# The merge of the key-value blocks into wo: from 48 split matmuls to 64 small float32 ones

## The chip, the cores and the metric

The kernel runs on one core of one Trainium2 chip. The metric is the device time of one execution in microseconds; a kernel's figure is the median of its runs.

## The reference

A linear-attention block and a gated feed-forward block share one input x of 2048 rows and 1024 columns, and the output joins them:

```python
xn = layernorm(x)
q, k, v = heads(xn @ wqkv)               # 32 heads of 32 columns
pq, pk = phi(q), phi(k)                  # phi(t) = t + 1 if t > 0 else exp(t), + 1e-6
kv  = einsum("hsd,hse->hde", pk, v)      # 32 x 32 for each head
den = einsum("hqd,hd->hq", pq, pk.sum(s)) + 1e-6
s = concat(pq @ kv / den) @ wo           # wo is 1024 x 1024
g = silu((silu(x @ w1) * (x @ w3)) @ w2) # 3584 hidden columns
out = x + s * g
```

All is float32. Since the division by den is by row and head, `(pq @ kv / den) @ wo` is `(pq / den) @ M`, where the 32 rows of M that belong to head h are `kv[h] @ wo[32h:32h+32]`. The kernel computes M, "the merge", once, and multiplies by it later.

## The kernel before

**Products.** The large products are made of 2x2 block products in seven multiplications (A11, S1 to S4, A12, A22 on one side; B11, B21, B22, T1 to T4 on the other). Each float32 operand is split into a high and a low part of the type fp32r: `split` casts on ACT (ScalarE) and subtracts on DVE (VectorE). `mm3` then multiplies high by high, high by low, low by high: three matmuls of 128x128 by 128x512 on PE (TensorE), the lines L109, L110 and L111.

**Order of the work.** The main line of the program is the projections and the two halves of the feed-forward block. Beside it runs a list of side jobs: `catch_up`, called at marks between products, takes one step of the first job of the list each time (a step ends at a `yield`). `go_on` runs a list of jobs one after another and has the loads of two jobs asked ahead. A job's tiles come from `job_tile`, one ring of four buffers; PSUM banks from `bank`, eight of them; split operands from `operand`, six. From the resulting program a scheduler sets the order of each engine's queue. All side jobs' loads and stores in question are issued by SP (SyncE).

**The stage of the change.** `attention_work` first divides 8 pieces of pq by den; then, for k = 0 to 3 and e = 0, 1, runs the pair `key_values(j)`, merge of j, with j = k + 4e (four heads, 128 rows of M each); then divides the other 24 pieces; then come sums of weights.

- `key_values(j)` loads g, the columns of xn^T pk that belong to four heads (an earlier product, 512 KB, L1309), and the same heads' columns of wqkv for v, wv (512 KB, L1312). L1323 makes the four heads' blocks, wv^T g, with 32 float32 matmuls that contract 128 of the 1024 rows each and have 32 columns, in four column tiles: `tile_position=(0, g * DH)`. The result is 128x32 in a bank `kv`: four 32x32 blocks stacked. L1327 multiplies on DVE with the 0/1 mask `hmask`, which spreads them to a 128x128 tile `kvf` with four blocks on the diagonal and zeros elsewhere.
- `merge_wo(k)` loads 128 rows of wo (L1340, 512 KB) for each e, splits `kvf` to `kvm`, and the two halves of wo's rows to `wos`, runs `mm3` into `wp` for each half, and copies the bank back over the rows of wo (L1356, ACT). After e = 1 it stores the four quarter blocks and their sums (`sums_of`, on POOL, lines L1145 to L1149) as 7 operands to `wp_d` (L1369, 256 KB each). The product by M loads `wp_d` (as `wpr`) some 300 us later.

The denominators (`den`, L1258) appear in the prediction for comparison: float32 matmuls in four column tiles of 128x32, with 256 columns each.

Of the kernel before, what the change touches and what calls it, by code (L numbers as in the profile page):

```python
# [9 lines left out]
F32 = mybir.dt.float32  # L10
FR = mybir.dt.float32r
# [5 lines left out]
P = 128  # L17
C = 512
# [4 lines left out]
def tile_linear_attention_times_swiglu(  # L23
# [10 lines left out]
    nc = tc.nc  # L34
    x, out = x[0], out[0]
    S, D = x.shape
    F = w1.shape[1]
    ND = D // P
# [52 lines left out]
    YS = ["Y00", "Y01", "Y10", "R5", "R2", "R4", "R6"]  # L91
    x_d = [dram.tile([P, TH // 2, len(XS), C], F32, name=f"x_d{h}") for h in range(NH)]
    y_d = [dram.tile([P, TH // 2, len(YS), ND // 2, P], F32, name=f"y_d{h}") for h in range(NH)]
    g_d = [dram.tile([P, ND // 2, C], F32, name=f"g_d{n}") for n in range(4)]
    a_d = {n: dram.tile([P, 2, ND // 2, C], F32, name=f"a_d{n}") for n in AOPS}

    def split(pair, src, negated=False):

        hi, lo = pair if isinstance(pair, tuple) else (pair[:, 0], pair[:, 1])
        if negated:  # L100
            nc.scalar.mul(hi, src, -1.0)  # L101
            return nc.vector.scalar_tensor_tensor(lo, src, -1.0, hi.bitcast(F32), op0=ALU.mult, op1=ALU.subtract)  # L102
        nc.scalar.copy(out=hi, in_=src)  # L103
        return nc.vector.tensor_sub(out=lo, in0=src, in1=hi.bitcast(F32))  # L104

    def mm3(acc, w, a, start, stop):

        (wh, wl), (ah, al) = w, a
        nc.tensor.matmul(acc, lhsT=wh, rhs=ah, start=start, stop=False, skip_group_check=True)  # L109
        nc.tensor.matmul(acc, lhsT=wh, rhs=al, start=False, stop=False, skip_group_check=True)  # L110
        return nc.tensor.matmul(acc, lhsT=wl, rhs=ah, start=False, stop=stop, skip_group_check=True)  # L111
# [10 lines left out]
    st = era1.enter_context(tc.tile_pool(name="st", bufs=2))  # L122
# [19 lines left out]
    def job_tile(shape, name):  # L142
        return praw.tile(shape, F32, tag="job", bufs=4, name=name)
# [66 lines left out]
    class Opening:  # L210
# [653 lines left out]
    def half(h):  # L864
# [47 lines left out]
        else:  # L912
# [318 lines left out]
    def go_on(work, ahead=2):  # L1231

        data = [j.load() for j in work[:ahead]]
        for i, j in enumerate(work):
            yield from j.steps(data[i])
            if i + ahead < len(work):
                data.append(work[i + ahead].load())
# [61 lines left out]

        return Job(load, steps)  # L1300

    kvf = {}

    def key_values(j):

        def load():
            g = job_tile([P, 2, ND // 2, P], f"g{j}")
            for e in range(2):
                nc.sync.dma_start(out=g[:, e], in_=g_d[2 * e + j % 2][:, :, j // 2 * P:(j // 2 + 1) * P])  # L1309
            w = job_tile([P, 2, ND // 2, P], f"wv{j}")  # L1310
            rows = wqkv[:, 2 * D + j * P:2 * D + (j + 1) * P]
            nc.sync.dma_start(out=w.rearrange("p e k n -> p (e k) n"), in_=rows.rearrange("(k p) n -> p k n", p=P))  # L1312
            return g, w

        def steps(both):
            yield True
            acc = bank(f"kv{j}")[:, :DH]
            g_, w_ = both
            for e in range(2):
                for k in range(ND // 2):  # L1320
                    for g in range(P // DH):
                        c = slice(g * DH, (g + 1) * DH)
                        nc.tensor.matmul(acc[c], lhsT=w_[:, e, k, c], rhs=g_[:, e, k, c], skip_group_check=True,  # L1323
                                         start=e + k == 0, stop=bool(e) and k == ND // 2 - 1, tile_position=(0, g * DH))
# [6 lines left out]
        return [Job(load, steps)]  # L1331

    def merge_wo(k):

        both = []

        def load(e):
            j = k + e * (ND // 2)
            t = job_tile([P, 2, C], f"wo{j}")
            nc.sync.dma_start(out=t, in_=wo[j * P:(j + 1) * P, :].rearrange("p (n c) -> p n c", c=C))  # L1340
            return t

        def steps(e, t):
            both.append(t)
            j = k + e * (ND // 2)
            kvm = st.tile([P, 2, P], FR, tag="kvm", bufs=1, name=f"kvm{j}")
            split(kvm, kvf[j])
            o = []
            for n in range(2):
                o.append(operand([P, 2, C], FR, f"wos{j}_{n}"))  # L1350
                split(o[n], t[:, n])
                yield True
            for n in range(2):
                acc = bank(f"wp{j}_{n}")
                mm3(acc, (kvm[:, 0], kvm[:, 1]), (o[n][:, 0], o[n][:, 1]), True, True)
                nc.scalar.copy(out=t[:, n], in_=acc)  # L1356
                yield True
            if e:
                b = [t[:, n] for t in both for n in range(2)]
                for n, i in (("B11", 0), ("B21", 2), ("B22", 3)):  # L1360
                    store(n, b[i])
                yield from sums_of(*b)
                for n, i in (("T1", 0), ("T3", 1), ("T4", 2), ("T2", 3)):
                    store(n, b[i])
                yield True

        def store(n, t):
            g, e = divmod(7 * k + PRODUCTS.index(n), 4)
            nc.sync.dma_start(out=wp_d[g][:, e], in_=t)  # L1369

        return [Job(lambda e=e: load(e), lambda t, e=e: steps(e, t)) for e in range(2)]
# [382 lines left out]
    for s, (i, c) in enumerate(STEPS):  # L1754
        p = ORDER[i]
# [11 lines left out]
        b, L = banks[c], lefts[s]  # L1767
# [7 lines left out]
        for negative, m, n in takes(p):  # L1775
            r = QT * c + m
# [36 lines left out]
```

## Time and profile before

| | us |
|---|---|
| median of 3 runs | 2263.31 (2262.43 to 2265.76) |
| the profiled execution | 2261.58 |
| its span | 2259.8 |
| PE busy in it | 2240.6 (99%) |
| DVE, ACT, POOL busy | 1553.4 (69%), 1044.8 (46%), 696.5 (31%) |
| first and last key-value matmul start | 1110.1, 1278.3 |
| first and last merge matmul start | 1120.9, 1293.6 |

The span is the profiled execution from its first to its last instruction. A row of a group gives line, engine, operation, output and inputs, their shapes, the count, busy us, mean ns of one, and the idle time ahead of it. Busy times of matmuls overlap, since they are pipelined: what one costs is the distance from its start to the next one's. A float32 matmul leaves two records, so "x16" at the denominators are eight. PEld is the weight loads, which run beside the matmuls. SPq is SyncE's queue of DMA issues.

### The profile page before, as it was taken

The numbers are of one execution on the slowest core, as the hardware profiler recorded it, in microseconds if no ns is written. First come the engines' busy times: TensorE is split into PE (matmuls) and PEld (weight loads), VectorE is DVE, ScalarE is ACT, GpSimd is POOL, SyncE is SP. The second block draws the span as 40 slices with busy tenths as digits, with TensorE's granted clock in tenths as the row PEclk, the third lists the DMA queues.
The fourth block names the chain that finished last, engine by engine and source line by source line (L and its number), as shares of the span: only waits on it lengthen the run. The fifth ranks groups of instructions, "written<-read, shape, count | busy, mean of one in ns | idle before, by whom it ended". The sixth has DMA issues, their size and how long they took to land.

```text
span 2259.8 us, 31282 instructions
## 1 busy us (share of the span) xinstructions
PE 2240.6 (99%) x10584; PEld 1844.9 (82%) x10584; DVE 1553.4 (69%) x2607; ACT 1044.8 (46%) x1780; POOL 696.5 (31%) x1163
## 2 busy tenths in 40 slices
PE   7999999999999999999999999999999999999998
PEld 6888888888888888778888888888888888888887
DVE  8987777665656776567766687856865555566576
ACT  6655454534343555434445443443522544444452
POOL 2220223377773621001244255478121000001010
PEclk9999999999999999999999999999999999999999
DMA  6555655677778745777766577877776856668595
GB/s 242 175 198 173 192 176 180 186 226 211 215 217 273 243 143 194 255 253 240 226 200 195 178 237 246 246 220 226 252 225 212 303 196 220 221 204 268 194 302 204
DMA packets 434657, 495.18 MB, mean 219 GB/s; under 512 B 22192, under 2 KB 328112, under 8 KB 434384
## 3 DMA queue, kind: packets, MB, share of 16 engines
q1 hardware_dynamic: 352112, 353.44, 49.4%
q0 software_dynamic: 26080, 82.99, 11.2%
q10 hardware_dynamic: 56304, 56.76, 8.0%
q8 instruction: 83, 1.36, 0.2%
q14 instruction: 78, 0.64, 0.1%
HBM read 315.62 MB, written 181.14 MB: 220 GB/s over the span
## 4 chain that ended last, share of the span: by engine, by line
PE 98%; DVE 1%; DMA 1%; issue 0%; ACT 0%; DVEq 0%
PE o L111 7%; PE o L110 7%; PE o L109 7%; PE g L109 2%; PE g L110 2%; PE g L111 2%; PE trk L716 1%; PE as L109 1%; PE ds L109 1%; PE cs L109 1%; PE ds L111 1%; PE cs L111 1%; PE as L110 1%; PE ds L110 1%; PE cs L110 1%; PE as L111 1%
## 5 line engine op out<-in xcount | busy, mean ns | idle before, releaser
L109 PE MATMUL o<-w,l 128*128 128x512 f32 x728 | 283.2, 389 | 0.0
L110 PE MATMUL o<-w,l 128*128 128x512 f32 x728 | 283.2, 389 | 0.0
L111 PE MATMUL o<-w,l 128*128 128x512 f32 x728 | 283.2, 389 | 0.0
L103 ACT CAST l<-lr 128x896 fp32r<-128x896 f32 (+1 forms) x106 | 98.5, 932 | 203.8 <-PE o L111 104.0
L104 DVE TENSOR_TENSOR l<-lr,l 128x896 fp32r<-128x896 f32 (+1 forms) x106 | 113.6, 1073 | 81.6 <-ACT l L103 80.3
L110 PEld LDWEIGHTS o<-w,l 128*128 128x128 f32 x728 | 136.6, 188 | 28.4
L109 PEld LDWEIGHTS o<-w,l 128*128 128x128 f32 x728 | 136.6, 188 | 28.4
L111 PEld LDWEIGHTS o<-w,l 128*128 128x128 f32 x728 | 136.6, 188 | 28.3
L1577 POOL DMA_DIRECT2D out<-acc x14 | 12.0, 860 | 397.6 <-DVE acc L1575 397.6
L104 DVE TENSOR_TENSOR xy<-xy,xy 128x512 fp32r<-128x512 f32 x112 | 73.1, 687 | 59.0 <-ACT xy L103 59.0
L103 ACT CAST xy<-xy 128x512 fp32r<-128x512 f32 x112 | 64.9, 620 | 96.2 <-PE g L111 74.2
L1787 DVE TENSOR_TENSOR acc<-o,acc 128x512 f32<-128x512 f32 x63 | 43.1, 690 | 87.9 <-PE o L111 87.9
L993 POOL TENSOR_TENSOR hs<-h,h 128x128 f32<-128x128 f32 x104 | 48.0, 482 | 142.1 <-DVE h L977 142.1
L110 PE MATMUL g<-xy,xy 128*128 128x512 f32 x224 | 87.5, 391 | 0.0
L111 PE MATMUL g<-xy,xy 128*128 128x512 f32 x224 | 87.2, 389 | 0.0
L109 PE MATMUL g<-xy,xy 128*128 128x512 f32 x224 | 80.5, 394 | 0.3 <-DVE gc L855 0.3
L993 POOL TENSOR_TENSOR hs<-h,hs 128x128 f32<-128x128 f32 (+1 forms) x130 | 73.6, 586 | 22.9 <-DMA h_d<-hs 20.0
L993 POOL TENSOR_TENSOR w2s<-w 128x256 f32<-128x256 f32 x75 | 54.4, 739 | 55.6 <-DMA wt_d<-w2s 54.5
L720 POOL DMA_DIRECT2D y_d<-y x48 | 34.6, 723 | 117.8 <-ACT y L747 43.0
L104 DVE TENSOR_TENSOR w<-wr,w 128x512 fp32r<-128x512 f32 x98 | 63.1, 686 | 11.1 <-ACT w L103 11.1
L103 ACT CAST w<-wr 128x512 fp32r<-128x512 f32 x98 | 57.8, 620 | 20.7 <-DMA wr<-in_B_w 15.2
L102 DVE SCALAR_TENSOR_TENSOR w<-wr,w 128x512 fp32r<-128x512 f32 x84 | 53.8, 687 | 4.1 <-ACT w L101 4.0
(5645 smaller groups left out, 6868.9 us busy)
## 6 DMA issues: line engine op xcount, KB each, us to landing
lr<-h_d SPq DMA_DIRECT2D x102, 448.0 KB
wr<-wt_d SPq DMA_DIRECT2D x126, 256.0 KB
wt_d<-w2s SPq DMA_DIRECT2D x50, 512.0 KB
h_d<-hs SPq DMA_DIRECT2D x96, 256.0 KB
w<-in_B_w SPq DMA_DIRECT2D x56, 256.0 KB
xy<-x_d SPq DMA_DIRECT2D x28, 512.0 KB
xy<-y_d SPq DMA_DIRECT2D x28, 512.0 KB
wr<-in_B_w SPq DMA_DIRECT2D x56, 256.0 KB
```

The lines of the kernel that those rows point to most:

```text
L102: return nc.vector.scalar_tensor_tensor(lo, src, -1.0, hi.bitcast(F32), op0=ALU.mult, op1=ALU.subtract)
L103: nc.scalar.copy(out=hi, in_=src)
L104: return nc.vector.tensor_sub(out=lo, in0=src, in1=hi.bitcast(F32))
L109: nc.tensor.matmul(acc, lhsT=wh, rhs=ah, start=start, stop=False, skip_group_check=True)
L110: nc.tensor.matmul(acc, lhsT=wh, rhs=al, start=False, stop=False, skip_group_check=True)
L111: return nc.tensor.matmul(acc, lhsT=wl, rhs=ah, start=False, stop=stop, skip_group_check=True)
L716: nc.tensor.transpose(p_[:, t * P:(t + 1) * P], src[:, t * P:(t + 1) * P], ident)
L720: nc.gpsimd.dma_start(out=y_d[h][:, :, YS.index(n), pair], in_=t.rearrange("p (t d) -> p t d", d=P))
L993: self.last = getattr(self.e, name)(**how)
L1577: nc.gpsimd.dma_start(out=out[rows, cols], in_=a, accum_op=ALU.add)
L1787: nc.vector.tensor_add(out=a, in0=b, in1=a)
```

## The change

The key-value blocks are no longer spread over a masked 128x128 tile. The eight `key_values` jobs now run one after another, and each copies its 128x32 result (`kvs`) and stores it to `kv_d` in DRAM, 16 KB. One load then brings all 32 blocks back as a tile `kv` of 128x256, in which the four heads of a group lie in different partitions than before. `merge_wo(kv, e, n)` is now four jobs: each loads 512 rows by 512 columns of wo in four pieces of 256 KB, arranged so that the 16 heads lie as four rows of tiles times four columns of tiles; it runs 16 float32 matmuls of 32x32 by 32x512, one for each head, in 16 tile positions, into four banks (`wp<e><n>_<r>`), with neither mask nor split; copies the four banks back on ACT; and stores them to `wm_d`. `merged_sums(k)`, four jobs of their own, load the merged blocks back from `wm_d` and do the sums and the stores to `wp_d` as before. The steps of these jobs are fewer, 59 instead of 72, so the divisions and sums of weights behind them come earlier among the marks. Lines in the new program are a few lower than in the old: `mm3` is L106 to L108, the loads of a key-value job L1304 and L1307, its matmul L1318.

```diff
-    hmask = const.tile([P, P], F32, name="hmask")
-    nc.vector.memset(hmask, 0.0)
-    for i in range(P // DH):
-        nc.vector.memset(hmask[i * DH:(i + 1) * DH, i * DH:(i + 1) * DH], 1.0)
...
+    kv_d = dram.tile([P // DH, DH, 2, P // DH, DH], F32, name="kv_d")
+    wm_d = [dram.tile([P, ND // 2, 2, C], F32, name=f"wm_d{e}") for e in range(2)]
...
     def key_values(j):
...
-            kvf[j] = st.tile([P, P], F32, tag="kvf", bufs=1, name=f"kvf{j}")
-            heads = [P, P // DH, DH]
-            nc.vector.tensor_mul(kvf[j].rearrange("p (g c) -> p g c", c=DH),
-                                 acc.unsqueeze(1).to_broadcast(heads), hmask.rearrange("p (g c) -> p g c", c=DH))
+            kv = st.tile([P, DH], F32, tag="kvs", name=f"kvs{j}")
+            nc.vector.tensor_copy(out=kv, in_=acc)
+            e, r = divmod(j, ND // 2)
+            nc.sync.dma_start(out=kv_d[r].rearrange("d e g c -> g d e c")[:, :, e], in_=kv)
             yield True
...
-    def merge_wo(k):
...
-            kvm = st.tile([P, 2, P], FR, tag="kvm", bufs=1, name=f"kvm{j}")
-            split(kvm, kvf[j])
-            o = []
-            for n in range(2):
-                o.append(operand([P, 2, C], FR, f"wos{j}_{n}"))
-                split(o[n], t[:, n])
-                yield True
-            for n in range(2):
-                acc = bank(f"wp{j}_{n}")
-                mm3(acc, (kvm[:, 0], kvm[:, 1]), (o[n][:, 0], o[n][:, 1]), True, True)
-                nc.scalar.copy(out=t[:, n], in_=acc)
-                yield True
...
+    def merge_wo(kv, e, n):
+
+        def load():
+            both = [job_tile([P, 2, C], f"wo{e}{n}_{i}") for i in range(2)]
+            rows = wo[e * C:(e + 1) * C, n * C:(n + 1) * C].rearrange("(r g d) c -> g r d c", g=P // DH, d=DH)
+            for g in range(P // DH):
+                nc.sync.dma_start(out=both[g // 2][:, g % 2], in_=rows[g])
+            return both
+
+        def steps(both):
+            yield True
+            accs = [bank(f"wp{e}{n}_{r}") for r in range(P // DH)]
+            for g in range(P // DH):
+                for r in range(P // DH):
+                    here = slice(r * DH, (r + 1) * DH)
+                    nc.tensor.matmul(accs[r][g * DH:(g + 1) * DH], lhsT=kv[here, e, g], rhs=both[g // 2][here, g % 2],
+                                     start=True, stop=True, skip_group_check=True, tile_position=(r * DH, g * DH))
+            for r, acc in enumerate(accs):
+                nc.scalar.copy(out=both[r // 2][:, r % 2], in_=acc)
+            yield True
+            for i in range(2):
+                nc.sync.dma_start(out=wm_d[e][:, 2 * i:2 * i + 2, n], in_=both[i])
+            yield True
+
+    def merged_sums(k):
+
+        def load():
+            both = [job_tile([P, 2, C], f"wm{e}_{k}") for e in range(2)]
+            for e, t in enumerate(both):
+                nc.sync.dma_start(out=t, in_=wm_d[e][:, k])
+            return both
...
     def attention_work():
         yield from go_on([divide(m, k) for m in range(2) for k in range(ND // 2)], 3)
-        work = []
-        for k in range(ND // 2):
-            for e, j in enumerate(merge_wo(k)):
-                work += key_values(k + e * (ND // 2)) + [j]
-        yield from go_on(work)
+        yield from go_on([key_values(j) for j in range(ND)])
+        kv = st.tile([P, 2, P // DH, DH], F32, tag="kv", bufs=1, name="kv")
+        nc.sync.dma_start(out=kv.rearrange("p e g c -> p (e g c)"), in_=kv_d.rearrange("r d e g c -> (r d) (e g c)"))
+        yield True
+        yield True
+        yield from go_on([merge_wo(kv, e, n) for e in range(2) for n in range(2)])
+        yield True
+        yield from go_on([merged_sums(k) for k in range(ND // 2)])
         yield from go_on([divide(m, k) for m in range(2, S // (2 * P)) for k in range(ND // 2)], 3)
```

More of the change, by code (lines that the diff above doesn't have):

```diff
@@ L1300, in divide @@
         return Job(load, steps)
-    kvf = {}
     def key_values(j):
@@ L1329, in steps @@
+            e, r = divmod(j, ND // 2)
+            nc.sync.dma_start(out=kv_d[r].rearrange("d e g c -> g d e c")[:, :, e], in_=kv)
             yield True
-        return [Job(load, steps)]
-    def merge_wo(k):
[L1335 to L1345, printed above, removed]
-            kvm = st.tile([P, 2, P], FR, tag="kvm", bufs=1, name=f"kvm{j}")
-            split(kvm, kvf[j])
-            o = []
-            for n in range(2):
-                o.append(operand([P, 2, C], FR, f"wos{j}_{n}"))
-                split(o[n], t[:, n])
-                yield True
-            for n in range(2):
-                acc = bank(f"wp{j}_{n}")
-                mm3(acc, (kvm[:, 0], kvm[:, 1]), (o[n][:, 0], o[n][:, 1]), True, True)
-                nc.scalar.copy(out=t[:, n], in_=acc)
-                yield True
[L1358 to L1365, printed above, removed]
@@ new lines, in key_values @@
+        return Job(load, steps)
+    def merge_wo(kv, e, n):
[19 more added lines that the diff above has]
+            yield True
+        return Job(load, steps)
@@ L1369, in store, with steps @@
             nc.sync.dma_start(out=wp_d[g][:, e], in_=t)
-        return [Job(lambda e=e: load(e), lambda t, e=e: steps(e, t)) for e in range(2)]
+        def steps(both):
+            yield True
+            b = [t[:, n] for t in both for n in range(2)]
+            for n, i in (("B11", 0), ("B21", 2), ("B22", 3)):
+                store(n, b[i])
+            yield from sums_of(*b)
+            for n, i in (("T1", 0), ("T3", 1), ("T4", 2), ("T2", 3)):
+                store(n, b[i])
+            yield True
+        return Job(load, steps)
     def all_denominators():
@@ L1379, in attention_work @@
         yield from go_on([divide(m, k) for m in range(2) for k in range(ND // 2)], 3)
-        work = []
-        for k in range(ND // 2):
-            for e, j in enumerate(merge_wo(k)):
-                work += key_values(k + e * (ND // 2)) + [j]
-        yield from go_on(work)
+        yield from go_on([key_values(j) for j in range(ND)])
+        kv = st.tile([P, 2, P // DH, DH], F32, tag="kv", bufs=1, name="kv")
+        nc.sync.dma_start(out=kv.rearrange("p e g c -> p (e g c)"), in_=kv_d.rearrange("r d e g c -> (r d) (e g c)"))
+        yield True
+        yield True
+        yield from go_on([merge_wo(kv, e, n) for e in range(2) for n in range(2)])
+        yield True
+        yield from go_on([merged_sums(k) for k in range(ND // 2)])
         yield from go_on([divide(m, k) for m in range(2, S // (2 * P)) for k in range(ND // 2)], 3)
```

## The prediction, made before the changed kernel ran

> **What bounds the kernel now.** I read the page's busy shares and its chain first, then TensorE's (PE's) waits, then a table by stage. From the page:
>
> ```profile
> span 2259.8 us, 31282 instructions
> PE 2240.6 (99%) x10584; PEld 1844.9 (82%) x10584; DVE 1553.4 (69%) x2607; ACT 1044.8 (46%) x1780; POOL 696.5 (31%) x1163
> PE 98%; DVE 1%; DMA 1%; issue 0%; ACT 0%; DVEq 0%
> ```
>
> All that PE waits for, and three stretches (columns: stretch, its length, then busy time and instructions of PE, of its weight loads, of DVE, ACT and POOL, the granted clock, the DMA share, GB/s):
>
> ```profile
> PE tA L296 <- ACT xa L285: 11.1, 2, 10.6
> PE g L109 <- DVE gc L855: 0.3, 1, 0.3
> ...
> 1111.00:1163.00 52.00, 52.00 (x349) 42.55 (x349) 30.91 (x50) 25.99 (x49) 23.08 (x39) 1.00 0.70 211
> 1163.00:1300.00 137.00, 137.00 (x904) 112.14 (x903) 88.14 (x144) 64.60 (x119) 43.06 (x61) 1.00 0.59 187
> 1300.00:1400.00 100.00, 100.00 (x443) 82.84 (x442) 84.43 (x167) 40.92 (x75) 55.41 (x92) 1.00 0.77 238
> ```
>
> PE is the chain. Its one large wait, 11.1 us, is for the first rows of x; in the stage of the change, 1110 to 1300, it is busy to the last hundredth. So each microsecond taken off PE's stream there is a microsecond off the end, and each that PE waits is lost one to one. An ordinary split matmul costs 100/443 = 0.226 us of the stream (its own 0.39 overlaps its neighbours). The granted clock is 1.00 throughout.
>
> **Removed: 48 fp32r matmuls.** The merge of before is three matmuls for each of 16 halves:
>
> ```profile
> L110 PE MATMUL wp<-wos,kvm 128*128 128x512 f32 x16 | 6.3, 395 | 0.0
> ...
> 1124.36 0.39 PE L109 MATMUL wp<-wos,kvm 128*128 128x512 f32 x1
> 1124.59 0.39 PE L110 MATMUL wp<-wos,kvm 128*128 128x512 f32 x1
> 1124.82 0.39 PE L111 MATMUL wp<-wos,kvm 128*128 128x512 f32 x1
> 1125.05 0.39 PE L110 MATMUL au__10258<-A,B21u__10274 128*128 128x512 f32 x1
> ```
>
> From the first start to that of the next product 0.69 us for three, 0.23 each: 48 x 0.23 = 11.0 us leave the stream.
>
> **Added: 64 float32 matmuls of 32x32, N=512, in four groups of 16.** No row shows 16 tiles. The nearest are the denominators (4 column tiles of 128x32, N=256, 8 matmuls in a group). Their neighbourhood, and the same group in four windows:
>
> ```profile
> 907.52 0.39 PE L111 MATMUL g<-xy,xy 128*128 128x512 f32 x1
> 907.83 1.07 PE L1258 MATMUL den<-pqd,zb 128*32 128x256 f32 x16
> 908.84 0.50 PE L109 MATMUL g<-xy,xy 128*128 128x512 f32 x1
> 909.18 0.40 PE L110 MATMUL g<-xy,xy 128*128 128x512 f32 x1
> ...
> L1258 PE MATMUL den<-pqd,zb x4: 403/403/403, 907.8 to 907.9; 128*32 128x256 f32 x4
> 907.83:908.07 0.24, 0.24 (x4) 0.16 (x8) 0.00 (x0) 1.00 1.01 128
> 908.07:908.29 0.22, 0.22 (x8) 0.13 (x4) 0.00 (x0) 1.00 0.81 177
> 908.29:908.51 0.22, 0.22 (x9) 0.13 (x4) 0.00 (x0) 1.00 0.78 158
> ```
>
> The eight matmuls leave 16 records, so a float32 matmul passes twice; four records begin together (the row for the first window alone), and the next window counts those four, still running, and four more. So four column tiles run side by side, in rounds of 0.22 us for 256 columns, 0.43 for 512. From 907.52 to 909.18 are 1.66 us, less the two ordinary matmuls 1.66 - 0.45 = 1.21; four rounds are 0.86, so going into the mode and out of it takes 0.35.
>
> If all 16 tiles run side by side, a group is two rounds of 0.43, 0.35 around them, and twelve more starts. The key-value row gives a start's price:
>
> ```profile
> 1109.80 0.39 PE L110 MATMUL dg__10063<-S,B22g__10113 128*128 128x512 f32 x1
> 1110.11 0.76 PE L1323 MATMUL kv<-g,wv 128*32 128x32 f32 x64
> 1110.81 0.51 PE L111 MATMUL dg__10063<-S,B22g__10113 128*128 128x512 f32 x1
> 1111.15 0.39 PE L109 MATMUL dg__10063<-S,B22g__10113 128*128 128x512 f32 x1
> ```
>
> 64 records in 0.76 us, at most 0.012 each: twelve are at most 0.14, and I take half, 0.07, since 16 columns per record are already part of that time. A group is 0.86 + 0.35 + 0.07 = 1.28 us, four are 5.1. The bounds: two rounds alone, 4 x 0.86 = 3.4 us; the four rows of tiles one after another, (4 x 0.86 + 0.35) x 4 = 15.2. I take the low part, since column tiles do run together in the nearest row and a row tile is nearer to a column tile than to a full matmul.
>
> Here a page speaks: the Trainium skill, "TensorE: Matmul & The Clock Gate", Part 3, puts 16 tiles of K=M=32, N=512 at 10.6 times the speed of one after another. By it a group would be 16/10.6 of one float32 matmul's 0.86, an estimate of 1.3 us, and the sum as above; no run shown so far has row tiles.
>
> **Kept: the key-value jobs.** From 1109.80 to 1111.15 one costs 1.35 - 0.45 = 0.90 us of the stream, eight before and eight after. What changes is where they stand.
>
> PE where the first merge stands. Before, in the middle of du1_1, its three matmuls in two pieces (kvm0 is the masked block, split; wos0_0 a split half of wo):
>
> ```order
> L111 MATMUL cu1_1__10289<-S3_1_6933,T3u1_1__10254 128x512
> L109 MATMUL au1_1__10258<-A12_1_6935,B21u1_1__10274 128x512
> L109 MATMUL wp0_0_10332<-wos0_0_10285,kvm0_10282 128x512
> L109 MATMUL du1_1__10290<-S1_1_6934,T1u1_1__10169 128x512
> L110 MATMUL du1_1__10290<-S1_1_6934,T1u1_1__10169 128x512
> L111 MATMUL du1_1__10290<-S1_1_6934,T1u1_1__10169 128x512
> L110 MATMUL wp0_0_10332<-wos0_0_10285,kvm0_10282 128x512
> ```
>
> The change, one stage later in du1_2, the first five rows of the group (four row tiles, four banks; the next three times four follow at once):
>
> ```order
> L108 MATMUL du1_2__10855<-S4_1_6934,B22u1_2__10932 128x512
> L1343 MATMUL wp00_0_11010<-wo00_0_10979,kv_10938 32x512
> L1343 MATMUL wp00_1_11011<-wo00_0_10979,kv_10938 32x512
> L1343 MATMUL wp00_2_11012<-wo00_0_10979,kv_10938 32x512
> L1343 MATMUL wp00_3_11013<-wo00_0_10979,kv_10938 32x512
> ```
>
> All eight key-value jobs now stand ahead of this: after the first they follow 24 to 36 ordinary matmuls apart, 24 x 0.226 + 0.90 = 6.3 us, where the chain before has them 20 and 30 apart:
>
> ```profile
> 1110.18 0.69 PE kv L1323 x50
> ...
> 1130.45 0.69 PE kv L1323 x50
> ...
> 1160.01 0.69 PE kv L1323 x50
> ```
>
> **Beside PE, at nothing.** ACT and DVE lose the splits and keep the 16 copies:
>
> ```profile
> L103 ACT CAST wos<-wo x16: 620/622/625, 1116.1 to 1287.0; 128x512 fp32r<-128x512 f32 x16
> L104 DVE TENSOR_TENSOR wos<-wo,wos x16: 681/692/807, 1116.8 to 1287.6; 128x512 fp32r<-128x512 f32 x16
> L104 DVE TENSOR_TENSOR kvm<-kvf,kvm x8: 280/293/643, 1116.2 to 1285.0; 128x128 fp32r<-128x128 f32 x8
> L1356 ACT COPY wo<-wp x16: 586/588/605, 1122.5 to 1294.3; 128x512 f32<-128x512 f32 x16
> ```
>
> ACT 16 x 0.62 = 9.9 us and eight short casts, DVE 16 x 0.69 + 8 x 0.29 = 13.4 us. PE waits for neither in the stage, so this gains nothing; it only covers that PE, 6 us earlier, asks for its operands 6 us earlier. The masked product and its five memsets go, eight small copies come, hidden likewise. The copies now come four in a row, 4 x 0.59 = 2.4 us, with four of eight banks held. The first matmul that waits for such a copy (eu1_3, for the last merge's second copy) stands 24 matmuls, 5.4 us, behind; 1.2 us of copies end before it. The sums on POOL (31% busy) are the same operations, later.
>
> SP gets more to issue: 8 stores of a key-value block, their one load, 8 more loads of wo (16 of 256 KB for 8 of 512), 8 stores and 8 loads of the merged halves, 33 in all. At
>
> ```profile
> L1309 SPq DMA_DIRECT2D g<-g_d x16: 529/577/707, 1099.5 to 1259.6; - x16
> L1312 SPq DMA_DIRECT2D wv<-in_A_wqkv x8: 382/612/1260, 1102.0 to 1260.4; - x8
> L1369 SPq DMA_DIRECT2D wp_d<-wo x28: 319/323/545, 1123.1 to 1300.3; - x28
> L103 ACT CAST wp<-wpr x28: 611/618/622, 1591.4 to 1620.0; 128x512 fp32r<-128x512 f32 x28
> ```
>
> 0.32 to 0.61 us each that is 11 to 20 us of SP in nearly 200. The merged halves have until 1591 to arrive, where the segment that multiplies them splits the first (the last row); they cost nothing unless they crowd others.
>
> SP at the loads, before (g and wv are the operands of a key-value job, wo the rows to merge, wp_d the stores of the merged):
>
> ```order
> L1340 DMA wo0_10178<-in_A_wo 128x1024
> L1309 DMA g4_10277<-g_d0_135 128x4x128
> L1309 DMA g4_10277<-g_d2_137 128x4x128
> L1312 DMA wv4_10280<-in_A_wqkv 128x8x128
> L1340 DMA wo4_10381<-in_A_wo 128x1024
> L1369 DMA wp_d0_85<-wo0_10178 128x512
> ```
>
> and after, where the load of a job waits on PE for the tiles of the job two before it:
>
> ```order
> L1304 DMA g3_10360<-g_d1_133 128x4x128 [waits DMAHW1_49,DMAHW2_49,DMAHW0_49,PE_49]
> L1323 DMA kv_d_129<-kvs1_10338 4x32x32 [waits DVE_49]
> L1304 DMA g3_10360<-g_d3_135 128x4x128 [waits DMAHW3_49]
> L1307 DMA wv3_10363<-in_A_wqkv 128x8x128 [waits DMAHW4_49]
> L1304 DMA g4_10440<-g_d0_132 128x4x128 [waits DMAHW6_49,DMAHW5_49,PE_49]
> L1304 DMA g4_10440<-g_d2_134 128x4x128
> L1307 DMA wv4_10443<-in_A_wqkv 128x8x128 [waits DMAHW7_49]
> ```
>
> The loads of wo between them are gone, and each job's 1 MB has two jobs' time, some 12 us, to arrive. At the stretch's 211 GB/s for a share of 0.70, 1 MB is 1.05/301 = 3.5 us of all the engines, so it fits if the others leave room. In 1111 to 1163 three to four jobs' loads are added and about 2 MB of stores go later, so 1.5 to 2 MB more in 52 us: the share rises from 0.70 to about 0.83.
>
> New on the path to the first merge is the round trip of the blocks. SP behind the last key-value job:
>
> ```order
> L1334 DMA wo01_0_10985<-in_A_wo 128x1x512
> L1323 DMA kv_d_129<-kvs7_10913 4x32x32
> L1334 DMA wo01_0_10985<-in_A_wo 128x1x512
> L1334 DMA wo01_1_10986<-in_A_wo 128x1x512 x2
> L1386 DMA kv_10938<-kv_d_129 128x256
> ```
>
> 54 ordinary matmuls, 12.2 us, stand on PE between that job and the merge that reads kv. The only DMAs of 1100 to 1300 whose landing the list of issues gives (KB each, us from issue to landing):
>
> ```profile
> qs_d<-qd POOLq DMA_DIRECT2D x2, 384.0 KB, 4.3
> qs_d<-qd POOLq DMA_DIRECT2D x2, 64.0 KB, 4.8
> ```
>
> Copy 0.3 (as the kvm row's), issue 0.4, landing 4.8, issue 0.4, landing 4.8: 10.7 us, 1.5 us inside the cover. If that cover goes, PE stands at wp00 for the excess, once.
>
> **Sum.** -11.0 + 5.1 = -5.9 us. On the profiled execution, 2261.58 (span 2259.8 and 1.8 around it), 2255.7; it lies 1.7 below the median of the runs, 2263.31, which goes to 2257.4, -0.26%. With the group's low bound it is -7.6, or 2255.7. What a measurement of this kernel tells from no change is 0.2%, 4.5 us.
>
> **Rivals.**
> - Row tiles take turns, only column tiles share a round: +15.2 - 11.0 = +4.2, 2267.5. For it: no row shows row tiles, and each reads other partitions into another bank. 0.10.
> - A tile's second pass holds the next tile's first, as starts in order would have it: 16 x 0.43 + 0.43 + 0.35 = 7.7 a group, 30.6, so +19.6, 2282.9. Against: the four windows, in which eight such matmuls would take 9 rounds, 1.94 us, and take 1.07. That matmuls start and end strictly in program order is the rule of the same part of the Trainium skill's TensorE page; the windows agree only for whole rounds. With all tiles wholly in series it would be near 2308. Together 0.03.
> - PE waits in the bunched stretch: the loads of kv3 to kv7 come late, or the round trip outlasts 12.2 us. For it: in the stretch the DMA share is 0.70 before what is added, SP issues 2 x 0.58 + 0.61 = 1.8 us per job and holds other stores between, and the margin at wp00 is 1.5 us. Against: the two-job lead of 12 us for 3.5 us of transfer. It cancels the gain at 5.9 us of wait in all, and is slower by over 0.2% from 10.4. As the mechanism that ends on the other side I price it as five key-value jobs late by 2.5 us each: 12.5 - 5.9 = +6.6, 2269.9. In all 0.24: 0.04 with waits under 1.4 us, still faster; 0.13 between; 0.07 slower.
> - The change gives nothing, since PE, 6 us early, finds DVE or a load not ready behind the stage: 2263.3. For it: DVE is 84% busy in 1300 to 1400. Against: it has lost 13 us of work just before. 0.05.
>
> **How the numbers follow.** The forecast has 0.58, its own range 2254.5 (the low bound less the runs' spread of about 1) to 2259.5. Faster by over 0.2%: 0.55 of these and 0.04 = 0.59. Same: 0.03 of the forecast, 0.13, 0.05, and 0.06 of the turns, which end beside the bound: 0.27. Slower: 0.07, 0.04, 0.03 = 0.14. The range goes up to 2267.5, where the turns end, and leaves out about 0.12 above and 0.05 below.
>
> **What would show it.** Right: a merge group as 32 records of one line within about 1.3 us, the next ordinary matmul starting some 1.4 us after the last one ahead of it; about 5.9 us less between the last matmul of the part that is alike ahead of 1110 and the first alike behind 1300; no new row among PE's waits. Wrong: wp groups of 3.8 us (turns) or 7.7 (order); PE waiting at kv for g or wv, or at the first wp for kv; gaps at the matmuls that follow a merge, for a bank.

## The result: 2333.8 us, 3.1% slower

The changed kernel takes 2333.8 us (2332.5 to 2334.6, 6 runs) against 2263.5 (2262.4 to 2265.8, 6 runs): a ratio of 1.0309, 95% interval 1.0296 to 1.0322. The forecast was 2257.4, the range ended at 2267.5.

From the page of the profile after:

```profile
span 2330.6 us, 31418 instructions
PE 2257.2 (97%) x10664; PEld 1848.0 (79%) x10664; DVE 1540.4 (66%) x2578; ACT 1033.4 (44%) x1756; POOL 691.8 (30%) x1163
DMA packets 440146, 503.84 MB, mean 216 GB/s; under 512 B 23457, under 2 KB 329505, under 8 KB 439873
```

DVE, ACT and POOL did a little less than before, the traffic rose by 8.7 MB, and PE idled: 2330.6 - 2257.2 = 73 us instead of 19. The largest of its waits (line, what released it; us in total, times, longest; du, dg, au, cu and the like are block products and sums of the main line):

```profile
PE tA L293 <- ACT xa L282: 11.3, 2, 10.8
PE wp L1343 <- issue: 9.6, 1, 9.6
PE du__11700 L106 <- DVE cu__11699 L669: 9.0, 1, 9.0
PE dg__13003 L106 <- DVE c22g__13048 L669: 7.2, 1, 7.2
PE wp L1343 <- DMA wo<-in_A_wo: 5.9, 3, 3.1
PE du__12070 L106 <- DVE cu__12069 L669: 4.8, 1, 4.8
PE au__12798 L106 <- DVE sT1u__12739 L482: 4.5, 1, 4.5
PE dg__12247 L106 <- DVE c22g__12292 L669: 4.2, 1, 4.2
```

Of these rows only the first was there before. The rows on `wp` are at the merges, those on DVE run on to 1480. Where the time went is read from the same matmul in both traces. Three places of before, of which the second is a matmul of du behind the eighth merge:

```profile
1160.63 0.51 PE L109 MATMUL cu__10705<-S,T3u__10673 128*128 128x512 f32 x1
...
1300.21 0.39 PE L111 MATMUL du__12017<-S,B22u__12056 128*128 128x512 f32 x1
...
1420.19 0.39 PE L109 MATMUL bg__13340<-S,T2g__13287 128*128 128x512 f32 x1
```

and the same three after:

```profile
1162.46 0.50 PE L106 MATMUL cu__10854<-S,T3u__10824 128*128 128x512 f32 x1
...
1340.09 0.63 PE L108 MATMUL du__12070<-S,B22u__12109 128*128 128x512 f32 x1
...
1490.96 0.39 PE L106 MATMUL bg__13387<-S,T2g__13331 128*128 128x512 f32 x1
```

1.8 us late at the first, 39.9 at the second, 70.8 at the third, and 70.8 to the end: 40 us are lost where the merges and the first divisions are, 31 where the other divisions are. The key-value jobs, bunched as they are, lost nothing: 1.8 us is the five more of them that stand ahead of that place (5 x 0.90) less the twelve merge matmuls that no longer do (12 x 0.23).

The merge group itself, in `spread13` below, where it does not wait:

```profile
1188.95 0.39 PE L108 MATMUL dg__11040<-S,T1g__10976 128*128 128x512 f32 x1
1189.27 1.14 PE L1343 MATMUL wp<-wo,kv 32*32 32x512 f32 x32
1190.34 0.50 PE L106 MATMUL ag__11019<-A,B21g__11035 128*128 128x512 f32 x1
1190.68 0.40 PE L107 MATMUL ag__11019<-A,B21g__11035 128*128 128x512 f32 x1
```

From 1188.95 to 1190.68 are 1.73 us, less 0.45 for two ordinary matmuls: 1.28 us, the forecast's figure. The arithmetic of a group on PE was right; what was lost are waits, and the slower clock behind them.

### The profile page after: what moved, and what is told of

Its sections match the earlier page's. It is cut to its first block, busy times and chain, and to the rows that moved or that the text cites. A ratio compares the mean times of both kernels' runs of the same rounds, so it can differ in the third digit from the quotient of the medians.

```text
span 2330.6 us, 31418 instructions
## 1 busy us (share of the span) xinstructions
PE 2257.2 (97%) x10664; PEld 1848.0 (79%) x10664; DVE 1540.4 (66%) x2578; ACT 1033.4 (44%) x1756; POOL 691.8 (30%) x1163
## 5 line engine op out<-in xcount | busy, mean ns | idle before, releaser
L108 PE MATMUL o<-w,l 128*128 128x512 f32 x728 | 283.3, 389 | 0.0
L106 PE MATMUL o<-w,l 128*128 128x512 f32 x728 | 283.3, 389 | 0.0
L106 PEld LDWEIGHTS o<-w,l 128*128 128x128 f32 x728 | 136.7, 188 | 28.3
L108 PEld LDWEIGHTS o<-w,l 128*128 128x128 f32 x728 | 136.7, 188 | 28.2
L108 PE MATMUL g<-xy,xy 128*128 128x512 f32 x224 | 87.2, 389 | 0.0
L106 PE MATMUL g<-xy,xy 128*128 128x512 f32 x224 | 80.5, 394 | 0.3 <-DVE gc L852 0.3
L1288 DVE SCALAR_TENSOR_TENSOR qd<-qd 128x512 f32<-128x512 f32 x32 | 23.6, 737 | 58.5 <-DMA qd<-pq_d 56.6
```

The costliest lines, as they stand in the source:

```text
L1288: nc.vector.scalar_tensor_tensor(t[:, :2], t[:, :2], 1e-6, t[:, 2:], op0=ALU.add, op1=ALU.mult)
```

## The experiments

### The divisions: which marks they fall on

In DVE's queue of before, the working instructions of successive divisions stand 10 to 13 instructions apart; of the changed kernel 23, 6, 8, 15, 10, 6, 20, 9, 6 and so on. A division has two steps, a first and a working one; 59 steps ahead of them instead of 72 is a shift by an odd number, 13, so that the working steps fall on marks on which the first steps fell. That is what parity means below. `pad1` has one empty step more, `pad12` and `pad13` 12 and 13:

```diff
+        for _ in range(1):      # 12, 13
+            yield True
         yield from go_on([divide(m, k) for m in range(2, S // (2 * P)) for k in range(ND // 2)], 3)
```

> The changed kernel with one more empty step between the merged sums and the 24 divisions (60 steps instead of 59 ahead of them). It loses 40 us against before by the place that was 1300 us there, and 31 us more by 1410, where the divisions run. Theory P (parity): a division has two steps and a group of products has six marks, so 59 instead of 72 steps ahead moves the working step of every division to the other half of the marks; DVE's queue then holds them in bunches and out of order, DVE waits 57 us for their loads, and PE behind it. One step more puts DVE's order back to one division every 10 to 13 instructions: about 31 us less, 2303 us, and DVE's wait for qd under 15 us. Rival C (crowding): the divisions start while the merged sums fill the DMA engines (share 0.92 in 1250 to 1300); one step, some 3 us later, changes nothing: 2330 to 2336 us.

> The changed kernel with 12 empty steps between the merged sums and the divisions (71 ahead of them): they start some 30 us later, clear of the merged sums, but on the same half of the marks as in the changed kernel. Theory P: still bunched, no gain beyond the start, 2325 to 2336 us. Rival C (crowding at the start): the 31 us come back, about 2303 us.

> As the one with 12, with 13 empty steps: the divisions stand exactly at the marks of before, 72 steps ahead of them. Theories P and C both: about 2303 us, the divisions' 31 us gone and the 40 us of the merges left. If it is well under the kernel with one empty step, part of the loss in the divisions is crowding as well.

Measured: 2293.2, 2327.0 and 2285.1 us. One step takes 40.6 us away; twelve, by which all divisions but the first two stand some 35 us later, take 6.8. So parity is the cause, and the start among the merged sums costs some 8 us beside it (pad1 against pad13). More than 31 us came back, since the first divisions lie ahead of the place that was 1300. DVE's wait for a division's loads between 1290 and 1500, in the changed kernel and then with one step more:

```profile
DVE qd L1288 <- DMA qd<-pq_d: 56.6, 7, 11.7
...
DVE qd L1288 <- DMA qd<-pq_d: 3.3, 2, 2.5
```

`odd` puts the same step into the kernel before, whose merge is untouched:

> The kernel before, with its own merge, and nothing changed but one empty step ahead of the 24 divisions (73 steps instead of 72). DVE's queue then holds the divisions bunched as in the changed kernel (gaps of 6 to 20 instructions instead of 10 to 13). Theory P: the loss behind 1300 has nothing to do with the merge, and one step makes it: 2290 to 2305 us, with DVE waiting over 40 us for qd's loads. Rival: the bunched order only hurts where PE was already late and the DMA crowded by the merged sums: 2263 to 2270 us.

Measured: 2305.0 us (2300.8, 2309.1). The wait of DVE between 1290 and 1500, before and with the step, and a stretch of both:

```profile
DVE qd L1291 <- DMA qd<-pq_d: 6.7, 4, 3.9
...
DVE qd L1291 <- DMA qd<-pq_d: 56.5, 8, 9.2
...
1310.00:1450.00 140.00, 140.00 (x619) 115.83 (x618) 118.94 (x237) 56.62 (x102) 73.35 (x118) 1.00 0.80 248
1310.00:1450.00 140.00, 119.42 (x492) 96.82 (x491) 100.80 (x194) 45.71 (x83) 64.25 (x112) 0.91 0.69 202
```

No engine has more to do; DVE holds what PE needs behind a division whose load is not there. About 41 us of the changed kernel's 70 come from the order of the divisions, and they come with either merge. Why the scheduler bunches DVE's queue at this parity stays open.

### The merges: spacing, then width

`spread13` spreads the 13 steps: four more ahead of the first merge, two after each of three merges, one after each of three merged sums.

> The changed kernel with the same 13 extra steps, but spread: four more between the key-value round trip and the first merge, two after each of the first three merges, one after each of the first three merged sums. Divisions at the marks of before. Theory S (spacing): the other 40 us are too little time for the round trip (PE waits 9.6 us at the first merge), for the loads of wo into two tiles that the merge before must first have stored, and for stores and sums that come bunched; with time between, PE waits under 10 us in all there and the kernel comes to 2258 to 2272 us. Rival B (bytes): 8 MB more through DRAM cost it whatever the spacing: about 2300 us.

Measured: 2262.0 us (2259.2 to 2264.7). It looked like spacing. Two kernels take its parts: `cover4` the four steps alone, `gaps6` the six (both with the rest ahead of the divisions).

> The changed kernel with 13 extra steps, four of them between the load of the blocks and the first merge, nine ahead of the divisions (the divisions at the marks of before). Against the kernel with all 13 ahead of the divisions (2285.1 us) only the first merge's lead differs: 108 ordinary matmuls behind the last key-value job instead of 54. Theory S: the wait of 9.6 us at the first merge and the slower clock right behind it go, 12 us, to about 2273. Rival: the wait only moves on to the loads of wo, 2281 us or more.

> The 13 extra steps as two after each of the first three merges and seven ahead of the divisions. The first merge keeps its short lead. Against 2285.1 us: theory S says that the waits for wo at the second to fourth merge go (6.3 us, and some 5 more of clock and late operands in the same stretch), to 2272 to 2276; the 9.6 us at the first merge stay. Rival B (bytes, the loads are slow whatever the spacing): 2283 us or more.

Measured: 2270.6 (2266.8 to 2272.3) and 2281.3 us. The lead of the first merge brings 14.5 us, the gaps only 3.8 of the 9 to 13 expected, though PE's wait for wo went: behind them, at the merged sums, 6.7 us of waits for ACT stood in place of 2.8. What makes the first merge late is seen on SP in the changed kernel, and on PE:

```profile
1163.69 3.36 SPq L1323 DMA_DIRECT2D kv_d<-kvs  x1
1167.10 7.03 SPq L1334 DMA_DIRECT2D wo<-in_A_wo  x3
1176.30 0.33 SPq L1386 DMA_DIRECT2D kv<-kv_d  x1
...
1184.58 2.02 PE L1343 MATMUL wp<-wo,kv 32*32 32x512 f32 x32 [9.56 <-issue]
```

Store to load 12.6 us, load to matmul 8.3. `kvpool` moves the load to POOL's queue, `kvrt` the stores too:

```diff
-            nc.sync.dma_start(out=kv_d[r].rearrange("d e g c -> g d e c")[:, :, e], in_=kv)
+            nc.gpsimd.dma_start(out=kv_d[r].rearrange("d e g c -> g d e c")[:, :, e], in_=kv)
...
-        nc.sync.dma_start(out=kv.rearrange("p e g c -> p (e g c)"), in_=kv_d...)
+        nc.gpsimd.dma_start(out=kv.rearrange("p e g c -> p (e g c)"), in_=kv_d...)
```

> The kernel with 13 extra steps ahead of the divisions, the one load of the key-value blocks issued by POOL's queue instead of SP's, where it stands behind three loads of wo (issued over 7 us, and ahead of it in the transfers). Theory Q (queue): the round trip itself is short, and PE's wait at the first merge falls from 9.6 us to under 3: about 2274 us. Rival L (landing): store and load take their 4 to 5 us each wherever they are issued, the wait stays over 6 us: 2281 us or more.

> The kernel with 13 extra steps ahead of the divisions (2285.1 us), with both the eight small stores of the key-value blocks and their load issued by POOL's queue. With the load alone there, PE still waited 7.5 us: the load was held until 1178.4, since the last small store, issued by SP at 1164.6 to 1167.2 behind the loads of wo, landed only then, and the load took 5.4 us. Theory Q2: the store is late because it stands behind SP's large transfers; on POOL's queue it lands in under 6 us, the round trip fits the 12.2 us and PE's wait is under 2 us: about 2274 us. Rival L2: a store of 128 pieces of 128 bytes is slow in itself, the wait stays over 5 us: 2280 us or more.

Measured: 2283.9 and 2280.9 us, against 2285.1. The load alone was not it: it waited for the store. With both on POOL the round trip is short:

```profile
1163.54 0.69 POOL L1323 DMA_DIRECT2D kv_d<-kvs  x1 [4.40 <-DVE kvs L1321]
1170.49 0.61 POOL L1386 DMA_DIRECT2D kv<-kv_d  x1 [6.25 <-DMA kv_d<-kvs]
...
1175.59 1.15 PE L1343 MATMUL wp<-wo,kv 32*32 32x512 f32 x32
...
1200.94 1.06 PE L1343 MATMUL wp<-wo,kv 32*32 32x512 f32 x8 [2.23 <-DMA wo<-in_A_wo]
```

The first merge no longer waits, so the store is slow by what stands ahead of it. But 8 us of the gain went to the third merge, which stands in pieces at 1196 to 1205 and waits for wo, 11 us of delay by the same matmuls (2.5 in `pad13`). The 2274 missed that. Two windows of the changed kernel, one ahead of and one inside the first wait:

```profile
1168.00:1174.00 6.00, 6.00 (x28) 4.95 (x28) 4.78 (x8) 1.48 (x3) 0.00 (x0) 1.00 0.35 110
1176.00:1184.50 8.50, 0.00 (x0) 0.00 (x0) 0.00 (x0) 0.00 (x0) 0.00 (x0) 0.59 0.33 115
```

and the DMA strip of its 1172 to 1183 in 40 slices (busy tenths, then GB/s):

```profile
DMA  2222222222222322222789722222222222222222
GB/s 97 97 101 104 104 97 104 104 104 91 95 77 90 101 97 112 97 104 104 216 305 350 233 102 97 112 89 97 104 97 97 104 97 97 112 89 97 104 97 93
```

PE waits for transfers, and the DMA engines are idle for two thirds of the time; but for one burst, which reaches 350 GB/s, some 100 GB/s flow. The loads of wo have four row groups as their outer dimension. `wide13`, `wide1` and `wide0` cut them the other way, on the kernels with 13, one and no extra steps:

```diff
-            rows = wo[...].rearrange("(r g d) c -> g r d c", g=P // DH, d=DH)
-            for g in range(P // DH):
-                nc.sync.dma_start(out=both[g // 2][:, g % 2], in_=rows[g])
+            rows = wo[...].rearrange("(r i g d) c -> r i d g c", i=2, g=2, d=DH)
+            for r in range(P // DH):
+                for i in range(2):
+                    nc.sync.dma_start(out=both[i][r * DH:(r + 1) * DH], in_=rows[r, i])
```

> The kernel with all 13 extra steps ahead of the divisions (2285.1 us), its loads of wo cut the other way: for each 32-row group a load with the 32 rows of a head as the outer dimension (eight of 128 KB), instead of four of 256 KB whose outer dimension is the 4 row groups. While the changed kernel waits for wo (1170 to 1183, 1224 to 1228) the DMA share stands at 0.2 to 0.25 with some 100 GB/s: as if four of sixteen engines worked. Theory N (narrow): such a load is spread over 4 engines, takes four times as long, and the small store and the load of the key-value blocks stand behind it; cut the other way, PE's waits at the merges fall from 16 us to under 4 and the kernel comes to 2258 to 2266 us with the steps as close as they were. Rival S (spacing alone): the same bytes as close together, 2278 to 2288 us.

> The same cut of the loads in the kernel with only one extra step (2293.2 us): the changed kernel with the two faults named so far taken away and nothing spread. Theory N: 2260 to 2272 us (the 8 us that the divisions lose by starting among the merged sums' stores may stay). Rival S: 2286 to 2296 us.

> The changed kernel with nothing but the loads of wo cut the other way (59 steps, the divisions bunched as in the changed kernel). The fourth corner to 2333.8 (neither fault mended), 2293.2 (parity mended) and 2269.5 (both). If the two faults add up, 2333.8 - 23.7 = 2310 us, within 4. If the wide loads alone gain much less than 23.7, PE's delay at the merges was partly hidden behind the divisions' delay; if much more, the narrow loads also held up the divisions.

Measured: 2262.7 (2260.0 to 2266.0), 2269.5 (2266.6 to 2272.0) and 2313.5 us (2310.9, 2316.2). The same bytes at the same steps, other loads, in the stretch that leads up to the first merge, and that merge:

```profile
1166.00:1171.00 5.00, 5.00 (x24) 4.14 (x23) 3.58 (x7) 1.18 (x2) 0.00 (x0) 1.00 1.07 295
...
1176.67 1.25 PE L1344 MATMUL wp<-wo,kv 32*32 32x512 f32 x32 [0.31 <-issue]
```

The share is full, and PE waits 0.31 us instead of 9.56. That four of sixteen engines carried the narrow loads is inferred from the share, 0.33 and less; no row names an engine. The Trainium skill's page "DMA: Bandwidth & Descriptors", section "Rules for kernel authors", says that a DMA uses at most as many engines as its access pattern's slowest dimension counts; four here, and these windows agree. Spacing had mainly given the narrow loads time. The round trip still takes as long as its cover, since seven issues of wo now stand on SP between store and load:

```profile
1164.38 0.53 SPq L1323 DMA_DIRECT2D kv_d<-kvs  x1
1164.96 9.13 SPq L1335 DMA_DIRECT2D wo<-in_A_wo  x7
1174.13 0.43 SPq L1387 DMA_DIRECT2D kv<-kv_d  x1
```

Store to load is 9.8 us here, load to matmul 2.5. The two faults nearly add (the two runs of `wide0` are 5 us apart):

| us | loads narrow | loads wide |
|---|---|---|
| parity of the changed kernel | 2333.8 | 2313.5 |
| one step more | 2293.2 | 2269.5 |
| 13 steps more | 2285.1 | 2262.7 |

### What was still missing against the forecast

With both mended, and the divisions at their old marks, 2262 to 2263 us are left, 5 above the forecast. In `wide13` they are lost at one place, the bunched merged sums. PE waits for ACT, and ahead of that ACT had stood for a store of a merged sum:

```profile
PE du__11716 L106 <- ACT T2g__11835 L469: 3.8, 1, 3.8
...
1255.46 0.63 ACT L970 ACTIVATE h<-c12g__11674 128x512 f32<-128x512 f32 x1 [4.30 <-DMA wp_d<-wm]
```

By the same matmuls PE is 6.0 us later behind this wait. The spread kernels lose theirs elsewhere. `spread11`, `spread15` and `spread19` place the steps otherwise; `widespread` has wide loads and the steps of spread13.

> As the kernel with the steps spread (2262.0 us, its runs from 2259.2 to 2264.7), but 11 extra steps: four at the first merge, two after each of three merges, none in the merged sums, one ahead of the divisions. In the spread kernel the stage of the merges alone came out 4.9 us shorter than before, as forecast, and 6.4 us were lost again at 1414, at one wait of PE for DVE, which waited for a store of h. Theory E (PE ahead of the divisions): the divisions' chain of loads and stores is a second bound that is met in some runs, here as well: 2258 to 2264 us, runs spread over 4 us or more. Rival: that loss was made by the merged sums' stores, and with other places of the steps it is gone: 2257 us, with a spread of 1 to 2.

> The spread kernel (four extra steps at the first merge, two after each of three merges, one after each of three merged sums) with two more ahead of the divisions: 15, the third of the three places that the divisions' working step can have among the six marks with DVE's order kept. Theory E: 2258 to 2264 us, the 5.6 us of the stage partly lost again behind 1300. If it comes to 2257 or 2258 with a small spread, the place among the marks decides and not PE's lead.

> The spread kernel with three steps instead of one after each of the first three merged sums: 19 extra, the divisions at the same of the six marks as before but one group of products later. The sums' 7 MB of stores get 16 us more. Theory E: as the others, 2258 to 2264 us. Rival (the sums' stores crowd what comes behind): 2256.5 to 2258.5 us.

> The same cut in the kernel with the 13 steps spread (2262.0 us, 2259.2 to 2264.7). Theory N: its late operands behind the merges came from narrow loads too only if they stood in the way of others; 2257 to 2262 us. It should not beat the kernel without the round trips (2258.8 us) by more than 1 us, since both have the same four groups on PE.

Measured: 2263.9 (2261.7 to 2267.3), 2261.3 (2259.5 to 2264.2), 2262.7 (2261.4 to 2265.6), 2262.1 us (2260.1 to 2264.0). No rival's 2257, and `widespread` ends at the upper edge of its range. In each profile the stage of the merges gains 3.5 to 6 us by 1300, by the same matmuls, and 3.4 to 6.4 are lost again between 1300 and 1570, at one to three waits of PE of 0.4 to 3.4 us and the slower clock behind the longer ones. For spread13 (its slowest run), and for widespread:

```profile
PE du__13148 L106 <- DVE cu__13147 L669: 3.4, 1, 3.4
...
PE du__13164 L106 <- DVE cu__13163 L669: 3.1, 1, 3.1
PE du__12408 L106 <- DVE cu__12407 L669: 1.0, 1, 1.0
```

Theory E, that a PE which is early must meet the divisions' own chain, was tested by `lean`: the kernel before with the two low matmuls of each merge left out.

> The kernel before with only the first of the three merge matmuls (high by high), the two low ones left out: nothing else is changed, no load, store, sum or step. 32 x 0.23 = 7.4 us less on PE between 1120 and 1294. Theory E: PE has less than that to spare over the divisions' chain behind the stage, so that part of what is taken off PE there comes back as waits between 1300 and 1450: 2258 to 2262 us, a gain of 1 to 5 us. Rival: the spread kernels lose their 5.6 us by their own new transfers and steps, and here all of it stays: 2255.5 to 2256.5 us.

Measured: 2255.3 us (2254.7 to 2257.1), ratio 0.9964, interval 0.9952 to 0.9977. All of the 7.4 stays; theory E falls as it was put, that any PE which is this early must meet the divisions. `bykey` keeps the 16-tile groups and drops both round trips (the two comments in the cut are added here):

```diff
+            for n in range(2):          # after the key-value matmuls of job j = k + 4e
+                to = slice((2 * e + n) * DH, (2 * e + n + 1) * DH)
+                for g in range(P // DH):
+                    nc.vector.tensor_copy(out=kvq[k][to, g], in_=acc[g * DH:(g + 1) * DH])
...
+            for e in range(2):          # merge of k: tile i holds heads 2i, 2i + 1
+                rows = wo[(k + e * (ND // 2)) * P:(k + e * (ND // 2) + 1) * P, :]
+                for i in range(2):
+                    for n in range(2):
+                        to = slice((2 * e + n) * DH, (2 * e + n + 1) * DH)
+                        nc.sync.dma_start(out=both[i][to], in_=rows[2 * i * DH:2 * (i + 1) * DH, n * C:(n + 1) * C].rearrange(
+                            "(g d) c -> d g c", d=DH))
...
+                for c in range(P // DH):
+                    here = slice(c * DH, (c + 1) * DH)
+                    nc.tensor.matmul(accs[c][g * DH:(g + 1) * DH], lhsT=kvq[k][here, g], rhs=both[g // 2][here, g % 2],
+                                     start=True, stop=True, skip_group_check=True, tile_position=(c * DH, g * DH))
...
+            work += [key_values(k), key_values(k + ND // 2), merge_wo(k)]
```

> The 16 float32 tiles without the round trips: for each k the two key-value jobs (k and k + 4), then one merge that uses both. DVE copies each 32x32 block from the bank to the two partition groups where it is wanted (8 copies a job), wo comes in by 32 partitions (8 loads of 128 KB for each k, the bytes of before), tile row c is the quarter block c = 2e + n, so that its bank is that block as the sums want it. Nothing of kv_d and wm_d is left; 18 steps for each k as before, the divisions at the marks of before. Theory S: what was wrong is where the changed kernel put its transfers and steps, not the matmuls: four groups of 1.28 us for 11.0 us, -5.9 us and no new wait of PE: 2256.5 to 2258.5 us. Rival: the spread kernels' 3 to 4 us of late operands behind 1300 come from the merges' four copies in a row on ACT and the four banks held: 2260 us or more here too.

Measured: 2258.8 us (2257.5 to 2260.3, 11 runs), ratio 0.9979, interval 0.9970 to 0.9988: faster than both kernels. Its merge group, its copies, and every wait of PE over 1 us behind the start:

```profile
1137.80 0.39 PE L106 MATMUL ag__10457<-A,B11g__10396 128*128 128x512 f32 x1
1138.12 1.14 PE L1351 MATMUL wp<-wo,kvq 32*32 32x512 f32 x32
1139.19 0.50 PE L104 MATMUL bg__10508<-S,T2g__10433 128*128 128x512 f32 x1
...
L1326 DVE COPY kvq<-kv x64: 169/186/197, 1111.7 to 1265.8; 32x32 f32<-32x32 f32 x64
...
PE kv L1318 <- DMA wv<-in_A_wqkv: 2.0, 1, 2.0
```

It is 0.3 us above its expectation, the wait at kv is one candidate for that: by the same matmuls PE is 4.4 us earlier behind the stage, with the 2.0 of that wait in it. So the forecast's price of the groups fits in a whole kernel. The 2.5 to 5 us that the kernels with round trips lack against `bykey` go with the round trips or with the order of the jobs, which `bykey` changes too (each k has its key-value jobs, its merge and its sums together); the runs do not part the two. What makes DVE late between 1330 and 1560 stays open.

## Why the prediction was wrong, step by step

- **"-11.0 + 5.1 = -5.9 us" on PE's stream: right.** The removed matmuls cost 0.23 each (lean: -8.0 us measured for 32, 7.4 by that price, the medians' noise of about 1 between); a group of 16 cost 1.28 us, as worked out. The rivals of turns and of starts in order fell: 1.28, not 3.8 or 7.7.
- **"Beside PE, at nothing": the step that failed most.** The text ahead of the prediction says that the divisions come at earlier marks, 59 steps instead of 72, and the prediction gave that no term. It was 40.6 us with narrow loads, 44.0 with wide ones (2313.5 - 2269.5). The order of DVE's queue shows it; the prediction read the order around the merges only. Its rival that PE finds DVE not ready behind the stage had the place, but for another reason (PE early), and could do no more than cancel the gain.
- **"Copy 0.3, issue 0.4, landing 4.8, issue 0.4, landing 4.8": mis-sized.** 10.7 us, counted from the copy, became 22.0: 1.1 to the store's issue, 12.6 to the load's, 8.3 to the matmul. The landings were priced by two rows of POOL's queue; on SP they stood behind narrow loads of wo. On POOL store to load took 7.0 us, and 5.1 more until the matmul; on SP with wide loads 9.8 and 2.5, 0.3 us over the cover.
- **The loads of wo, "16 of 256 KB for 8 of 512": counted as issues on SP only.** Their shape was not looked at. It cost 20.3 us (2333.8 - 2313.5) to 23.7 (2293.2 - 2269.5), by way of that round trip and of the other merges' own loads.
- **"The share rises from 0.70 to about 0.83": right, and not what decided.** It was 0.87 in 1111 to 1163, and at the key-value loads, which the prediction had named as the risk, PE waited at most 0.7 us in any kernel that keeps their order. In the wait at the first merge the share was 0.33: the bandwidth was there and was not used.
- **The rival "PE waits in the bunched stretch"** had the place at wp00 and the sign, at a price of 12.5 us and a chance of 0.24. "Each that PE waits is lost one to one" was too little: the wait of 9.56 us cost 10.8 (below). This rival and the missed divisions were two mechanisms, and their prices add; the rivals had been priced one at a time.
- **The merged sums, "the same operations, later"**: they came bunched, and some 7 us were lost where the divisions began among their stores (2269.5 against 2262.7 with wide loads); in `wide13` one wait at a store of theirs cost another 6.0.

## What to carry to other kernels

When work is regrouped, the arithmetic on the busiest engine is the easy part: read the order of every in-order queue as far behind the edit as steps are counted from it, since one step more or less can reorder work that the edit does not touch. Look at the shape of each new load, not only its bytes: a transfer that is waited for while the DMA share is low may be narrow; cutting the loads of wo the other way, for the same bytes, gained 20 to 24 us here. Price a round trip through DRAM by what stands ahead of it in its own queue, and first ask whether small copies between partition groups replace it, as 64 of 0.19 us did in `bykey`.

## What the runs showed of the hardware that I had not expected

After a wait PE is slow. Two windows of the changed kernel, right behind the 9.56 us and then on:

```profile
1184.50:1188.00 3.50, 3.42 (x36) 1.55 (x37) 0.00 (x0) 1.24 (x3) 0.00 (x0) 0.54 0.00 0
1188.00:1195.00 7.00, 7.00 (x33) 5.75 (x32) 3.37 (x5) 4.13 (x9) 2.17 (x3) 1.00 0.64 217
```

The granted clock is 0.54 for 3.5 us, and the group takes 2.02 us instead of 1.14. By the same matmuls PE falls 11.6 us behind at this merge; `kvrt`, which does not wait there, falls 0.8 behind. So the wait of 9.56 us cost 10.8. In `spread13` a wait of 3.4 us cost 6.4. The Trainium skill's "TensorE: Matmul & The Clock Gate", section "Why this matters for your kernels", warns of gaps over about 3 us; the trace agrees for this one. Over the whole changed kernel PE was busy 2257.2 us, 16.6 more than before, with 5.9 us less to do.
